# Building a selector matrix earlier on the Pool engine, and reordering two kinds of DMA on SyncE, in a sliding-window attention and GeGLU kernel

## The chip, the cores and the metric

The kernel runs on one core of a Trainium2 chip. The metric is the device time in microseconds (us) of one execution. Before the change three runs gave 400.01, 400.31 and 400.64 us; their median is 400.31 us. One further execution was recorded by the hardware profiler; all rows of the profile come from that one.

## The reference

For 8 batches of 8 heads, 576 positions and head size 64 the reference computes causal attention in a window of 128 positions with a linear (ALiBi) bias, and feeds the result, 4608 tokens of 512, through a gated feed-forward layer:

```python
scores = scale * np.matmul(q, k.transpose(0, 1, 3, 2))
mask = (rel >= 0) & (rel < window)                  # window = 128
scores = np.where(mask, scores + bias[None], -1e9)
attn = softmax(scores)
x = np.matmul(attn, v)  ->  (4608, 512)
g, val = x @ w_gate, x @ w_val                      # (512, 1536) each
out = (gelu(g) * val) @ w_out                       # (1536, 512)
```

Inputs and output are 32-bit floats in DRAM.

## The kernel before

**Loads.** The Pool engine issues all loads (`load`, `load_w`): five DMAs for each of q, k and v of a batch, which convert to bf16 on the way, and the weights, in four slices of 384 columns each for the gate (`wg`) and the value (`wv`) matrix, then two pieces of `wo`. The buffers `qs`, `ks`, `vb` exist twice; batch b uses number b mod 2, so a load of batch b + 2 waits until batch b has been read.

**Transposes.** q and k are needed with the head dimension on the partitions (`qT`, `kT`). Batches 0 and 1 are transposed by TensorE through an identity matrix (`transpose`, line 105). Batches 2 to 7 are transposed by two DMAs that SyncE issues (`transposes_dma`, line 113).

**Attention.** `scores2` and `scores` compute keys times queries (line 121), ScalarE takes the exponential (line 128), VectorE multiplies a mask with the bias in it (line 131). `sums` adds the probabilities of each query with a matrix of ones (line 176), and VectorE takes the reciprocal into `sumrow`, a tile "r" (line 185). The reciprocal has to be spread over 64 partitions for each head, into a tile "rb". For batches 0 to 3 TensorE does this with the selector matrix `sel` (`spread_pe`, matmul at line 199 and copies at line 206). For batches 4 to 7 DMAs do it: one writes r to a DRAM tile "rd", two read it back broadcast (`spread_dma`, lines 189 and 191). `values` multiplies the probabilities with v (line 217), and VectorE multiplies by rb into `xT` (line 223).

**Feed-forward.** A group g is 512 tokens; there are nine. `gate_val` does eight matmuls for one of 12 blocks of 128 hidden columns (line 236), gelu on ScalarE (line 240) and the product on VectorE (line 241). `out_half` does six matmuls for half of the contraction of 128 tokens (line 252); after the second half ScalarE copies the result into a tile "osb" (line 257) and SyncE sends it out (line 259). The pool of osb has three buffers. All PSUM tiles come in turn from one pool of eight banks: `gate_val` takes two banks for each block, `out_half` one for two halves.

**Order.** The order of instructions on each engine is the order in which the program is written (`manual_schedule`); each engine works its list from the front, and an instruction whose operand is not ready holds everything behind it on that engine. The same is so for the lists of DMAs on SyncE and Pool. The first batch's attention is written out by hand, then comes a loop over the groups: `transposes_dma(g + 2)` and `load_v(g + 2)`, the 12 blocks of `gate_val`, `load_qk(g + 3)`, and then the eight halves of `out_half` mixed with the attention of coming batches by the lists `todo` and `steps`. In groups 3 to 6 `sums` and `spread_dma` of batch g + 1 stand behind block 0, and its `values` behind blocks 8 and 10.

Of the kernel before, what the change touches and what calls it, by code (L numbers as in the profile page):

```python
# [10 lines left out]
ALU = mybir.AluOpType  # L11
# [15 lines left out]
def kernel(  # L27
# [10 lines left out]
    nc = tc.nc  # L38
    B, H, S, D = q.shape
# [23 lines left out]
    def bank():  # L63
        return psum.tile([128, 512], FP32, name="ps")
# [8 lines left out]
    sel = consts.tile([128, 2, 64], FP32, name="sel")  # L73
# [7 lines left out]
    def load(t, src, b, js=range(5)):  # L81
        for j in js:
            lo = 64 if j == 0 else 0
            nc.gpsimd.dma_start(  # L84
                out=t[lo:128, j, :].rearrange("p (h d) -> p h d", h=H),
                in_=src[b][:, 128 * j - 64 + lo:128 * j + 64, :].rearrange("h p d -> p h d"))

    def load_qk(b):
        load(qs[b % 2], q, b)
        load(ks[b % 2], k, b)  # L90

    def load_v(b):
        load(vb[b % 2], v, b)
# [7 lines left out]
    def transpose(b, what, c, js, ps):  # L101

        src, dst = ((ks, kT), (qs, qT))[what]
        for n, j in enumerate(js):
            nc.tensor.transpose(  # L105
                out=ps[:, 128 * n:128 * n + 128],
                in_=src[b % 2][:, j, 128 * c:128 * c + 128], identity=ident)
        return (dst[b % 2][:, js[0]:js[0] + len(js), c, :],
                ps[:, 0:128 * len(js)].rearrange("p (j t) -> p j t", t=128))

    def transposes_dma(b):
        for src, dst in ((ks, kT), (qs, qT)):
            nc.sync.dma_start_transpose(  # L113
                out=dst[b % 2].rearrange("p j c t -> p (j c) t"),
                in_=src[b % 2].rearrange("p j x -> p (j x)"))
# [29 lines left out]
    def scores(b, s, cs):  # L145

        pss = []
        for c in cs:
            ps = [bank(), bank()]
            pss.append(ps)  # L150
            for j, blocks, col in (((0, (0, 1), 0), (1, (1, 2), 256)),
                                   ((4, (4,), 0), (2, (3,), 128), (3, (3, 4), 256)))[s]:
                for i in (0, 1):
                    score(b, c, i, j, blocks, ps[i], col)
        for c, ps in zip(cs, pss):
            P = p_pool[s].tile([128, 2, 512], BF16, name="P")
            probs[b, s, c] = P
            for i in (0, 1):
                exp(P[:, i, :], ps[i])
            mask(P.rearrange("p i (n x) -> p i n x", n=2),  # L160
                 emask[:, 2 * c:2 * c + 2, :].unsqueeze(2).to_broadcast((128, 2, 2, 256)))
# [8 lines left out]
    def sums(b, s):  # L170

        ps = bank()
        for j, a, e in PIECES[s]:
            for i in (0, 1):
                for c in range(4):
                    nc.tensor.matmul(  # L176
                        out=ps[32 * c:32 * c + 32, a:e],
                        lhsT=ones[:, min(j, 1), i, :], rhs=prob(b, s, c, i, j, e - a),
                        start=(i == 0 and j == 2 * s), stop=(i == 1 and j == 2 * s + 2),
                        skip_group_check=True)  # L180
        if s == 0:
            sumrow[b] = r_pool.tile([128, S], FP32, name="r")
            recip[b] = r_pool.tile([128, 4, S], FP32, name="rb")
        lo, hi = PART[s]
        nc.vector.reciprocal(sumrow[b][:, lo:hi], ps[:, 0:hi - lo])  # L185

    def spread_dma(b):
        d = d_pool.tile([4, 2, S], FP32, name="rd")
        nc.sync.dma_start(out=d.rearrange("c i s -> (c i) s"), in_=sumrow[b][0:128:16, :])
        for i in (0, 1):  # L190
            nc.sync.dma_start(
                out=recip[b][64 * i:64 * i + 64, :, :],
                in_=d[:, i, :].unsqueeze(0).to_broadcast((64, 4, S)))
# [14 lines left out]
    def values(b, s, cs):  # L208
        lo, hi = PART[s]
        pss = []  # L210
        for c in cs:
            ps = bank()
            pss.append(ps)
            for j, a, e in PIECES[s]:
                for i in (0, 1):
                    h = 2 * c + i
                    nc.tensor.matmul(  # L217
                        out=ps[64 * i:64 * i + 64, a:e],
                        lhsT=vb[b % 2][:, j, 64 * h:64 * h + 64],
                        rhs=prob(b, s, c, i, j, e - a),  # L220
                        start=(j == 2 * s), stop=(j == 2 * s + 2), skip_group_check=True)
        for c, ps in zip(cs, pss):
            nc.vector.tensor_tensor(  # L223
                out=xT[:, c, b * S + lo:b * S + hi], in0=ps[:, 0:hi - lo],
                in1=recip[b][:, c, lo:hi], op=ALU.mult)
# [3 lines left out]
    def gate_val(g, f, lo=0, hi=512):  # L229
        if g not in hid:  # L230
            hid[g] = h_pool.tile([128, NF, 512], BF16, name="hT")
        t0 = 512 * g
        pg, pv = bank(), bank()
        for w, ps in ((wg, pg), (wv, pv)):
            for c in range(4):
                nc.tensor.matmul(  # L236
                    out=ps[:, 0:hi - lo], lhsT=w[:, c, 128 * f:128 * (f + 1)],
                    rhs=xT[:, c, t0 + lo:t0 + hi], start=(c == 0), stop=(c == 3))
        gl = g_pool.tile([128, 512], BF16, name="gelu")
        nc.scalar.activation(out=gl[:, 0:hi - lo], in_=pg[:, 0:hi - lo], func=AF.Gelu)  # L240
        nc.vector.tensor_tensor(out=hid[g][:, f, lo:hi], in0=pv[:, 0:hi - lo],  # L241
                                in1=gl[:, 0:hi - lo], op=ALU.mult)
# [20 lines left out]
    for t in qs + ks:  # L263
        nc.vector.memset(t[0:64, 0, :], 0.0)
    nc.gpsimd.affine_select(
        out=ident, in_=ident, compare_op=ALU.not_equal, fill=1.0,
        base=0, pattern=[[-1, 128]], channel_multiplier=1)
# [3 lines left out]
    for half, base, step, chan in ((0, 0, 1, -1), (1, -1, -1, 1)):  # L271
        t = tmpl[:, 128 * half:128 * half + 128]
        nc.gpsimd.affine_select(
            out=t, in_=t, compare_op=ALU.is_ge, fill=1e9,
            base=base, pattern=[[step, 128]], channel_multiplier=chan)
    for js in ((0, 1, 2), (3, 4)):
        for j in js:
            for t, src in ((qs[0], q), (ks[0], k)):
                load(t, src, 0, (j,))
    load_v(0)  # L280
    step = DFF // 4
    for n in range(4):
# [5 lines left out]
    for i in range(2):  # L288
        nc.vector.memset(ones[64:128, 0, i, 16 * i:16 * i + 16], 1.0)
        nc.vector.memset(ones[:, 1, i, 16 * i:16 * i + 16], 1.0)  # L290
    nc.vector.memset(sel, 0.0)
    for i in range(2):
        nc.vector.memset(vb[i][0:64, 0, :], 0.0)
    for h in range(H):
# [10 lines left out]
    for (w, c), ps in pss.items():  # L305
        (act, dve)[w](out=(kT, qT)[w][0][:, 0:3, c, :],
                      in_=ps[:, 0:384].rearrange("p (j t) -> p j t", t=128))
# [10 lines left out]
    scores(0, 0, (2, 3))  # L318
    rest((2, 3), dve)
    scores(0, 1, (0, 1))  # L320
    for c in range(4):
        nc.gpsimd.affine_select(  # L322
            out=sel, in_=sel, compare_op=ALU.not_equal, fill=1.0,
            base=-32 * c, pattern=[[-16, 2], [0, 64]], channel_multiplier=1)
    sums(0, 0)
    scores(0, 1, (2, 3))
    spread_pe(0, 0)
# [9 lines left out]
    for n in range(2):  # L337
        nc.gpsimd.dma_start(
            out=wo[:, 6 * n:6 * n + 6, :],
            in_=moe_w_out[768 * n:768 * n + 768, :].rearrange("(c p) f -> p c f", p=128))  # L340
# [20 lines left out]
    def steps(g):  # L361
        b = g + 2
        if g in todo:
            return todo[g]
        if b >= B:
            return range(8)
        return [("s2", b), ("s", b, 0, (0, 1)), 0, 1, ("s", b, 0, (2, 3)), 2, 3,
                ("s", b, 1, (0, 1)), 4, 5, ("s", b, 1, (2, 3)), 6, 7]
# [3 lines left out]

    for g in range(NG):
        if g + 2 < B:
            transposes_dma(g + 2)
            load_v(g + 2)
        for f in range(3 if g == 0 else 0, NF):
            gate_val(g, f)
            if g == 0 and f >= 8:
                for w in (0, 1):  # L380
                    o, i = transpose(1, w, f - 8, range(5), bank().bitcast(BF16))
                    (act, dve)[w](out=o, in_=i)  # L382
            if 3 <= g < B - 1:
                if f == 0:
                    sums(g + 1, 0)
                    sums(g + 1, 1)
                    spread_dma(g + 1)
                elif f in (8, 10):
                    for s in (0, 1):
                        values(g + 1, s, (f - 8, f - 7))  # L390
        if g + 3 < B:
            load_qk(g + 3)
        for item in steps(g):
            if isinstance(item, int):
                out_half(g, item)
            else:
                RUN[item[0]](*item[1:])
# [30 lines left out]
```

## Time and profile before

| what | value |
|---|---|
| median of three runs | 400.31 us |
| the profiled execution's own time | 402.94 us |
| its span, first to last instruction | 401.1 us |
| TensorE matmuls (PE) busy | 352.8 us, 88% |
| VectorE (DVE) busy | 188.4 us, 47% |
| ScalarE (ACT) busy | 187.7 us, 47% |
| GpSimd (POOL) busy | 110.9 us, 28% |
| share of the chain that ended last: PE / DMA / ACT / POOL | 76% / 7% / 6% / 5% |

A row of the timeline has the start and length in us, the engine, the line, the operation with output and inputs, and the count; in brackets stands how long the engine was idle before it and what ended that. "SPq" is the list of DMAs on SyncE: the length of a row there is how long SyncE was held by issuing, and landing comes later. A row of the waits has who waited for whom, the total in us, the number of times and the longest. A row of the DMA view has output and input, the issuing list, the number, the size and the median us from issue to landing. A row of the windows has a stretch, its length, each engine's busy us with a count, the clock that TensorE was granted (1.00 is full), the busy share of the DMA engines and GB/s.

### The profile page before, as it was taken

The page shows a single profiled execution, that of the slowest core. Times are in us where ns is not written, and L with a number is a line of the kernel's source. Part 1 is how long each engine was busy: PE and PEld are TensorE (multiplying, and loading weights), DVE is VectorE, ACT ScalarE, POOL GpSimd, SP SyncE. Part 2 cuts the span into 40 slices and gives each one's busy share as a digit, 9 for nine tenths or more (in the row PEclk, how much of TensorE's full clock was granted, in tenths as well). Part 3 has the DMA queues.
Part 4 walks back from the last instruction along what each step waited for, and adds up shares of the span by engine and source line. Part 5 has one row for each costly group of instructions (what it writes and reads, how often), then busy time and mean ns, then how long its engine had stood idle before and what let it go on. Part 6 is the DMA issues. An engine that isn't in the chain of part 4 may idle for free.

```text
span 401.1 us, 6564 instructions
## 1 busy us (share of the span) xinstructions
PE 352.8 (88%) x2616; PEld 172.4 (43%) x2616; DVE 188.4 (47%) x308; ACT 187.7 (47%) x337; POOL 110.9 (28%) x142
## 2 busy tenths in 40 slices
PE   2700899879998999899959999999999999999996
PEld 1500555444444444444434445444444444444442
DVE  2630544483448744877344556464556521321420
ACT  3820334844368644676308633953584222323321
POOL 9945864727300560173029002100000000000000
PEclk9955799999999999999978999999999999999999
DMA  9999999999991899299949983977020502002002
GB/s 69 148 202 163 147 163 180 141 98 134 134 91 54 80 151 134 38 114 150 148 94 150 175 173 41 104 133 171 2 78 32 117 26 78 2 27 79 2 4 100
DMA packets 156863, 41.40 MB, mean 103 GB/s; under 512 B 144512, under 2 KB 150144, under 8 KB 156832
## 3 DMA queue, kind: packets, MB, share of 16 engines
q0 software_dynamic: 118304, 18.88, 65.0%
q1 hardware_dynamic: 38528, 22.10, 26.1%
q8 instruction: 20, 0.33, 0.3%
q14 instruction: 11, 0.09, 0.1%
HBM read 42.47 MB, written 9.51 MB: 130 GB/s over the span
## 4 chain that ended last, share of the span: by engine, by line
PE 76%; DMA 7%; ACT 6%; POOL 5%; DVE 2%; SPq 2%; issue 1%; POOLq 0%; DVEq 0%; ACTq 0%
PE ps L236 43%; PE ps L252 22%; PE ps L217 4%; ACT P L128 4%; DMA wv<-in_moe_w_val_dram 4%; PE ps L121 3%; DMA rb<-rd 2%; SPq L113 2%; PE ps L176 2%; PE ps L199 2%; POOL ks L84 1%; POOL qs L84 1%; POOL vb L84 1%; ACT L128 1%; DVE r L185 1%
## 5 line engine op out<-in xcount | busy, mean ns | idle before, releaser
L241 DVE TENSOR_TENSOR hT<-ps,gelu 128x512 bf16<-128x512 f32 (+2 forms) x111 | 74.2, 674 | 122.7 <-PE ps L236 110.7
L240 ACT ACTIVATE gelu<-ps 128x512 bf16<-128x512 f32 (+2 forms) x111 | 64.9, 586 | 126.1 <-PE ps L236 123.7
L236 PE MATMUL ps<-xT,wg 128*128 128x512 bf16 (+2 forms) x444 | 113.2, 377 | 0.5 <-DVE xT L223 0.2
L236 PE MATMUL ps<-xT,wv 128*128 128x512 bf16 (+2 forms) x444 | 112.3, 376 | 0.0
L252 PE MATMUL ps<-wo,hT 128*128 128x512 bf16 x432 | 99.5, 380 | 0.0
L128 ACT ACTIVATE P<-ps 128x512 bf16<-128x512 f32 x144 | 74.3, 629 | 9.7 <-PE ps L121 9.6
L131 DVE TENSOR_TENSOR P<-P,emask 128x1024 bf16<-128x1024 bf16 x72 | 49.0, 686 | 36.9 <-ACT P L128 36.6
L84 POOL DMA_DIRECT2D vb<-in_v_dram x40 | 33.7, 868 | 116.9 <-PE ps L217 116.8
L236 PEld LDWEIGHTS <-wv 128*128 128x128 bf16 x444 | 43.5, 98 | 51.0 <-issue 1.3
L236 PEld LDWEIGHTS <-wg 128*128 128x128 bf16 x444 | 42.2, 98 | 49.4 <-issue 1.9
L252 PEld LDWEIGHTS <-hT 128*128 128x128 bf16 x432 | 39.6, 98 | 48.8 <-issue 4.4
L257 ACT COPY osb<-ps 128x512 f32<-128x512 f32 x36 | 21.7, 602 | 40.1 <-PE ps L252 34.3
L84 POOL DMA_DIRECT2D qs<-in_q_dram x40 | 34.0, 874 | 19.7 <-PE ps L105 7.4
L84 POOL DMA_DIRECT2D ks<-in_k_dram x40 | 34.1, 895 | 3.5 <-DMA wv<-in_moe_w_val_dram 2.1
L185 DVE RECIPROCAL r<-ps 128x320 f32<-128x320 f32 (+1 forms) x16 | 30.7, 1938 | 0.9 <-PE ps L176 0.9
L199 PE MATMUL ps<-r,sel 32*128 32x320 f32 (+1 forms) x64 | 6.8, 493 | 25.8 <-POOL sel L322 21.0
L223 DVE TENSOR_TENSOR xT<-ps,rb 128x320 bf16<-128x320 f32 (+1 forms) x64 | 24.8, 449 | 9.2 <-DMA rb<-rd 9.2
L121 PE MATMUL ps<-qT,kT 64*128 64x256 bf16 (+1 forms) x384 | 24.2, 255 | 0.7 <-DVE qT L382 0.4
L217 PE MATMUL ps<-P,vb 128*64 128x128 bf16 (+2 forms) x384 | 19.9, 258 | 4.5 <-DVE xT L223 4.5
L217 PEld LDWEIGHTS <-vb 128*64 128x64 bf16 x384 | 16.2, 117 | 11.5 <-issue 11.3
L121 PEld LDWEIGHTS <-kT 64*128 64x128 bf16 x384 | 13.7, 97 | 15.0 <-issue 12.5
L206 ACT COPY rb<-ps 128x320 f32<-128x320 f32 (+1 forms) x16 | 5.7, 417 | 24.6 <-PE ps L199 24.6
(37 smaller groups left out, 93.1 us busy)
## 6 DMA issues: line engine op xcount, KB each, us to landing
out_dram<-osb SPq DMA_DIRECT2D x36, 256.0 KB, 2.1
rb<-rd SPq DMA_DIRECT2D x8, 576.0 KB, 7.1
qs<-in_q_dram POOLq DMA_DIRECT2D x32, 128.0 KB, 5.5
ks<-in_k_dram POOLq DMA_DIRECT2D x32, 128.0 KB, 6.0
vb<-in_v_dram POOLq DMA_DIRECT2D x32, 128.0 KB, 4.3
wg<-in_moe_w_gate_dram POOLq DMA_DIRECT2D x4, 384.0 KB, 11.9
wv<-in_moe_w_val_dram POOLq DMA_DIRECT2D x4, 384.0 KB, 13.1
wo<-in_moe_w_out_dram POOLq DMA_DIRECT2D x2, 768.0 KB, 9.3
```

Source lines behind the costliest of these rows:

```text
L84: nc.gpsimd.dma_start(out=t[lo:128, j, :].rearrange("p (h d) -> p h d", h=H), in_=src[b][:, 128 * j - 64 + lo:128 * j + 64, :].rearrange(" ...
L121: nc.tensor.matmul(out=ps[:, col:col + 128 * n].rearrange("p (n t) -> p n t", n=n), lhsT=kT[b % 2][lo:lo + 64, j, c, :], rhs=qT[b % 2][lo: ...
L128: nc.scalar.activation(out=dst, in_=src, func=AF.Exp, scale=0.125)
L131: nc.vector.tensor_tensor(out=dst, in0=dst, in1=m, op=ALU.mult)
L185: nc.vector.reciprocal(sumrow[b][:, lo:hi], ps[:, 0:hi - lo])
L217: nc.tensor.matmul(out=ps[64 * i:64 * i + 64, a:e], lhsT=vb[b % 2][:, j, 64 * h:64 * h + 64], rhs=prob(b, s, c, i, j, e - a), start=(j == ...
L223: nc.vector.tensor_tensor(out=xT[:, c, b * S + lo:b * S + hi], in0=ps[:, 0:hi - lo], in1=recip[b][:, c, lo:hi], op=ALU.mult)
L236: nc.tensor.matmul(out=ps[:, 0:hi - lo], lhsT=w[:, c, 128 * f:128 * (f + 1)], rhs=xT[:, c, t0 + lo:t0 + hi], start=(c == 0), stop=(c == 3))
L240: nc.scalar.activation(out=gl[:, 0:hi - lo], in_=pg[:, 0:hi - lo], func=AF.Gelu)
L241: nc.vector.tensor_tensor(out=hid[g][:, f, lo:hi], in0=pv[:, 0:hi - lo], in1=gl[:, 0:hi - lo], op=ALU.mult)
L252: nc.tensor.matmul(out=po, lhsT=hid[g][:, f, 128 * t:128 * (t + 1)], rhs=wo[:, f, :], start=(f == 0), stop=(f == NF - 1))
L257: nc.scalar.copy(out=osb, in_=po)
```

## The change

Two independent edits. The first builds `sel` (a zero fill on VectorE and four `affine_select` on Pool) right behind the loads of q and k of batch 0, ahead of the loads of v and the weights; before, the four stood on Pool behind all weights and the q and k loads of batch 1. The second leaves the order in groups 0 to 2 as it is, but in groups 3 to 5 writes `transposes_dma(g + 2)` behind `spread_dma(g + 1)` instead of at the head of the group. No instruction is added or removed.

```diff
             for t, src in ((qs[0], q), (ks[0], k)):
                 load(t, src, 0, (j,))
+    nc.vector.memset(sel, 0.0)
+    for c in range(4):
+        nc.gpsimd.affine_select(
+            out=sel, in_=sel, compare_op=ALU.not_equal, fill=1.0,
+            base=-32 * c, pattern=[[-16, 2], [0, 64]], channel_multiplier=1)
     load_v(0)
...
-    nc.vector.memset(sel, 0.0)
...
     scores(0, 1, (0, 1))
-    for c in range(4):
-        nc.gpsimd.affine_select(
-            out=sel, in_=sel, compare_op=ALU.not_equal, fill=1.0,
-            base=-32 * c, pattern=[[-16, 2], [0, 64]], channel_multiplier=1)
     sums(0, 0)
...
         if g + 2 < B:
-            transposes_dma(g + 2)
+            if g < 3:
+                transposes_dma(g + 2)
             load_v(g + 2)
...
                     spread_dma(g + 1)
+                    if g + 2 < B:
+                        transposes_dma(g + 2)
```

On Pool, at the start of the program (qs_94, ks_96 and vb_102 are the buffers of batch 0, ks_97 and vb_103 of batch 1), the two places of the difference are these:

```order
 L84 DMA qs_94<-in_q_dram 128x8x64
 L84 DMA ks_96<-in_k_dram 128x8x64
+L282 AFFINE_SELECT sel<-sel 128x128 x4
 L84 DMA vb_102<-in_v_dram 64x8x64
 L84 DMA vb_102<-in_v_dram 128x8x64 x4
```

and, 23 DMAs further down,

```order
 L84 DMA ks_97<-in_k_dram 64x8x64
 L84 DMA ks_97<-in_k_dram 128x8x64 x4
-L322 AFFINE_SELECT sel<-sel 128x128 x4
 L338 DMA wo<-in_moe_w_out_dram 128x6x512 x2
 L84 DMA vb_103<-in_v_dram 64x8x64
```

The four selects moved past 23 DMAs: the five of v, the eight of wg and wv and the ten of q and k of batch 1.

On SyncE, from the outputs of group 2 to those of group 3, the list before is:

```order
L259 DMA out_dram<-osb 128x512 x4
L113 DMA_TRANSPOSE kT_101<-ks_97 128x20x128
L113 DMA_TRANSPOSE qT_99<-qs_95 128x20x128
L189 DMA rd<-r 8x576
L191 DMA rb<-rd 64x4x576 x2
L259 DMA out_dram<-osb 128x512 x4
```

and with the change:

```order
L259 DMA out_dram<-osb 128x512 x4
L189 DMA rd<-r 8x576
L191 DMA rb<-rd 64x4x576 x2
L113 DMA_TRANSPOSE kT_101<-ks_97 128x20x128
L113 DMA_TRANSPOSE qT_99<-qs_95 128x20x128
L259 DMA out_dram<-osb 128x512 x4
```

The three DMAs that spread the reciprocal now stand ahead of the two transposes, which therefore also stand behind the spread's waits: for the reciprocal, and for rd to land. Groups 4 and 5 change in the same way; group 6 has no transposes and stays.

## The prediction

> **What bounds the kernel now.** I read the page's shares first: TensorE is busy 88% of the span, and its chain covers 76%. Only its idle time and its slow time can be won. The list of waits names the two idle times that this change touches.
>
> ```profile
> span 401.1 us, 6564 instructions
> PE ps L199 <- POOL sel L322: 21.0, 1, 21.0
> DVE xT L223 <- DMA rb<-rd: 9.2, 3, 7.8
> PE ps L217 <- DVE xT L223: 4.5, 1, 4.5
> ```
>
> One wait of 21.0 us is for the selector; one of 4.5 us is for a multiply that itself waits for rb. The second edit can touch three groups (3, 4, 5), but only one of them stops TensorE. The timeline (PE, DVE, POOL, then the chain) shows the first wait.
>
> ```profile
> 19.40 0.74 PE L121 MATMUL ps<-qT,kT 64*128 64x128 bf16 x12
> 41.11 1.45 PE L199 MATMUL ps<-r,sel 32*128 32x320 f32 x8 [20.97 <-POOL sel L322]
> 42.49 2.13 PE L217 MATMUL ps<-P,vb 128*64 128x192 bf16 x24
> 64.70 0.44 PE L105 MATMUL ps<-ident,ks 128*128 128x128 bf16 x5
> ...
> 20.85 2.15 DVE L185 RECIPROCAL r<-ps 128x320 f32<-128x320 f32 x1
> ...
> 39.64 1.42 POOL L322 TENSOR_SCALAR_AFFINE_SELECT sel<-sel 128x128 f32<-128x128 f32 x4
> ...
> 20.04 16.70 DMA wv<-in_moe_w_val_dram
> ```
>
> The matmul needs r and sel. r is ready at 20.85 + 2.15 = 23.00; sel comes at 41.1 because its four instructions stand behind loads that wait for weights still landing.
>
> **Edit one: sel earlier.** The selects now stand 23 DMAs ahead, long before 23.0, so what ends last is the reciprocal. The matmul starts at 23.04 (r plus 0.04 of hand-over), not 41.11: **18.07 us** sooner. I then asked what is late next.
>
> *Weights and k.* The selects hold Pool 1.42 us, so each load behind them lands at most 1.42 later, until the place they left, which gives the 1.42 back ahead of wo. These rows give the tightest cases, first the start of wv's first slice, then issue to landing of that slice and of a piece of k of batch 1:
>
> ```profile
> 15.63 0.86 POOL L97 DMA_DIRECT2D wv<-in_moe_w_val_dram  x1
> ...
> wv<-in_moe_w_val_dram POOLq DMA_DIRECT2D x1, 384.0 KB, 9.6
> ...
> ks<-in_k_dram POOLq DMA_DIRECT2D x1, 128.0 KB, 5.6
> ```
>
> The first wv slice lands at 15.63 + 9.6 + 1.42 = 26.7. Its first user follows the spread by 2.13 + 1.45 us of older matmuls and four of its own block, so not before 27. The last wv piece lands at 20.04 + 16.70 + 1.42 = 38.2; its user, block 9, stands behind the first transposes on TensorE, at 64.70 - 18.07 = 46.6. Those transposes need the last piece of k, issued at 38.75 (ahead of the selects, 0.89 before 39.64): 38.75 + 5.6 + 1.42 = 45.8, 0.8 early. Nothing is lost, on paper: 0, with a bound of +1.5.
>
> *The clock.* The windows show what idleness does to TensorE's clock.
>
> ```profile
> 21.00:22.00 1.00, 0.00 (x0) 0.00 (x0) 1.00 (x1) 1.00 (x3) 0.00 (x0) 0.73 1.30 198
> ...
> 45.00:46.00 1.00, 1.00 (x7) 0.66 (x6) 0.16 (x1) 0.31 (x1) 1.00 (x3) 0.82 1.22 194
> ```
>
> Work ended at 20.14; the granted clock drops within 21 to 22 and returns within 45 to 46, about 4.3 us after work resumed. That slow work is paid either way if the remaining gap, 20.14 to 23.04, still drops it; the history up to 22 is the same, so I take no gain. The Trainium skill ("TensorE: Matmul & The Clock Gate", Part 1: The HAM clock gate) says that the clock is halved after an idle window of about 3.4 us and that the windows run free. By that rule a gap of 2.9 us need not halve it. The trace differs here: it fell some 1.4 us into the gap. Bound: -2.0 us, since half of 4.3 us at half clock would be won.
>
> *SyncE's list at the end of group 0.* TensorE comes 18 us sooner to the outputs; SyncE does not. Its first two entries are the transposes of batch 2, and behind them stand the outputs of group 0.
>
> ```profile
> 64.93 3.92 SPq L113 DMA_TRANSPOSE kT<-ks  x1
> 79.55 16.84 SPq L259 DMA_DIRECT2D out_dram<-osb  x4
> 96.61 5.55 SPq L113 DMA_TRANSPOSE kT<-ks  x1
> 102.33 8.52 SPq L113 DMA_TRANSPOSE qT<-qs  x1
> ...
> 72.35 4.20 POOL L84 DMA_DIRECT2D qs<-in_q_dram  x5 [7.44 <-PE ps L105]
> ...
> 95.44 0.59 ACT L257 COPY osb<-ps 128x512 f32<-128x512 f32 x1 [3.12 <-issue]
> ...
> 95.36 19.87 PE ps L236 x92
> ...
> out_dram<-osb SPq DMA_DIRECT2D x1, 256.0 KB, 6.0
> ...
> qT<-qs SPq DMA_TRANSPOSE x1, 14.0
> ```
>
> The transposes of batch 2 start when its k has landed, at 64.93; that follows Pool's loads and stays near 65. But the loads of batch 3, held until 72.35 by TensorE's transposes, now run on at once and collide with them. The pair at 96.61, beside such loads, held SyncE for 5.55 + 8.52 us and some 0.2 between. So the first output, ready at 79.55 - 18.07 = 61.5, is issued at about 65 + 14.3 = 79.3 and lands 6.0 later (the out row, beside loads), at 85.3. The fourth osb copy, due at 95.44 - 18.07 = 77.4, reuses the first one's buffer (three exist) and waits until then; ScalarE's gelus queue behind it. TensorE goes on from 77.2 with the banks it has: 28 matmuls at 19.87 / 92 = 0.216, to 83.2; the next needs the bank that the copy frees at 85.9: 2.7 us idle. Then the first gelu (1.28 of table loading and 0.60, as at the other group starts) lets it wait another 0.8. I take **+3.5**. Below: 0, where SyncE is held for about 8 us as at 64.93. Above: the last transpose lands 14.0 after its issue and the output behind it, copy at 88.6, with a clock drop: +9.
>
> **Edit two: the spread ahead of the transposes.** Group 3 (DVE, SPq, chain, PE) and, for comparison, group 4:
>
> ```profile
> 185.10 3.76 DVE L185 RECIPROCAL r<-ps 128x320 f32<-128x320 f32 x2
> ...
> 181.17 7.19 SPq L113 DMA_TRANSPOSE kT<-ks  x1
> 188.53 6.84 SPq L113 DMA_TRANSPOSE qT<-qs  x1
> 195.46 0.71 SPq L189 DMA_DIRECT2D rd<-r  x1
> ...
> 198.36 7.92 DMA rb<-rd
> ...
> 201.44 1.03 PE L236 MATMUL ps<-xT,wv 128*128 128x512 bf16 x4
> 206.95 2.02 PE L217 MATMUL ps<-P,vb 128*64 128x192 bf16 x24 [4.48 <-DVE xT L223]
> 212.43 0.90 PE L121 MATMUL ps<-qT,kT 64*128 64x128 bf16 x16
> ...
> 228.97 3.76 DVE L185 RECIPROCAL r<-ps 128x320 f32<-128x320 f32 x2
> ...
> 227.01 3.21 SPq L113 DMA_TRANSPOSE kT<-ks  x1
> 230.32 3.06 SPq L113 DMA_TRANSPOSE qT<-qs  x1
> ...
> 247.00 1.13 PE L217 MATMUL ps<-P,vb 128*64 128x192 bf16 x24
> 249.90 0.83 PE L121 MATMUL ps<-qT,kT 64*128 64x128 bf16 x16
> ...
> kT<-ks SPq DMA_TRANSPOSE x1, 5.2
> ...
> qT<-qs SPq DMA_TRANSPOSE x1, 5.5
> ```
>
> r is ready at 188.86, but SyncE is held by transposes until 195.37; rb lands at 206.28, and TensorE stands from 202.47 to 206.95. With the spread first, rd goes out at 188.9 and rb lands 206.28 - 195.46 = 10.8 later, at 199.7: the stop of 4.48 goes. So does the slow work behind it: from the second values to the scores it took 212.43 - 206.95 = 5.48 in group 3 and 249.90 - 247.00 = 2.90 in group 4, the same instructions. Together 4.48 + 2.58 = **7.06 us** sooner. In groups 4 and 5 rb already stops nothing.
>
> What is late next: kT and qT, whose first user is the scores of batch g + 2 (212.43 - 7.06 = 205.37 in group 3). Undisturbed, a pair lands about 3.3 + 5.5 = 8.8 after its first issue (230.32 - 227.01, and the last row, qT of group 0; kT of group 4 took 5.2), of which I put down 2 as start-up, from rd: 195.46 to the next issue at 197.64, leaving 6.8 of moving. I estimate that it moves behind rb: group 3: 188.9 + 10.8 + 6.8 = 206.5, late by 1.2. Group 4: 232.73 + 10.8 + 6.8 = 250.35 against 249.90, late by 0.45; group 5 is built alike, 0.45. Sum **+2.1**. Below 0, since the 2 us are rough; above, the pair as slow as at 96.61, in the rivals.
>
> **Sum.** 402.94 - 18.07 + 3.5 - 7.06 + 2.1 = 383.4 for an execution like the profiled one. The runs' median was 2.63 below it: **380.8 us**.
>
> **Rivals.**
>
> (a) *No new wait* at either place: 380.8 - 5.6 = 375.2. For it: both are worked out from rows with other neighbours. Against it: the loads do move up. 0.15.
>
> (b) *The clock stays full* through the 2.9 us gap: 378.8. 0.10; the row at 21 to 22 speaks against it.
>
> (c) *The jam at the end of group 0 at its upper bound*, 9 instead of 3.5: 386.3. 0.15.
>
> (d) *The wait moves*: rb and the transposes share the engines instead of queueing. rb has some 6 us of moving, of which about 1.6 are done when the transposes start; 4.4 at half speed lands it 4.4 later, at 204.1 in group 3 and 248.0 in group 4. TensorE resumed 0.67 after rb (206.95 against 206.28), so it stops 2.3 us in group 3 (from 202.47) and some 1.6 each in groups 4 and 5: 5.5 instead of 2.1, and with a clock drop of 2.6 or two: 384 to 389. 0.07. The Trainium skill ("DMA: Bandwidth & Descriptors", Queues, rings and completion order) says that each DMA engine consumes one issuer's descriptors in ring order, which speaks against (d); no row here isolates it.
>
> (e) *Slower*: the transposes late in all of groups 3, 4 and 5. If each pair took what the one at 96.61 took, 102.33 + 14.0 - 96.61 = 19.7 instead of 8.8, the scores would wait 10.9 more and run into a slow clock (2.6), three times: 380.8 + 40.5 = 421. The change turns slower once a pair exceeds about 13 us. Against it: Pool's loads for batch g + 3 are mostly done when these transposes now start. 0.03.
>
> **How the numbers follow.** My forecast case holds 0.50. Faster by over 0.2% (what a measurement of this kernel can tell from no change) holds in all but (e): 0.96 with a little of (e)'s lower end; same 0.01; slower 0.03. The range 375 to 388 takes in (a), (b), (c) and most of (d).
>
> **What would show it.** Right: no wait on sel; the first line 199 at 23; a wait of the fourth osb copy for an output DMA near 77; no wait of line 223 for rb in group 3; short waits of line 121 for the transposes in groups 3 to 5. Wrong: TensorE waiting for wv or k between 26 and 47, a stop at the values of groups 3 to 5, or long waits at the scores.

## The result, and the profile after

The changed kernel ran in 382.25 us (median of 4 executions, 380.54 to 383.15), the kernel before in 400.48 (4 executions, 400.01 to 400.93): a ratio of 0.954, 95% interval 0.9501 to 0.9579. The forecast was 380.8, within 375 to 388. The profiled execution of the changed kernel took 382.87 us. One of the later executions of the kernel before took 410.91 us in a slower state of the chip; the ratios and ranges below leave it out.

The list of waits of the changed kernel shows what has gone and what has come (who waits for whom, total, times, longest):

```profile
PE ps L199 <- DVE r L185: 5.2, 3, 3.0
...
PE ps L236 <- ACT osb L257: 2.5, 1, 2.5
```

The wait of 21.0 us for `sel` is gone; line 199 now waits 3.0 us at most, for the reciprocal. TensorE's wait of 4.5 us at line 217 is gone. Two waits of TensorE are new: 2.5 us behind a copy into osb, which itself waited 10.9 us for an output DMA, and 0.5 us for a transpose (the rows of these come further down).

The timeline of the changed kernel, PE from the first spread on:

```profile
23.00 1.45 PE L199 MATMUL ps<-r,sel 32*128 32x320 f32 x8 [3.00 <-DVE r L185]
...
36.57 1.03 PE L236 MATMUL ps<-xT,wg 128*128 128x512 bf16 x4
46.93 0.44 PE L105 MATMUL ps<-ident,ks 128*128 128x128 bf16 x5
```

The spread starts at 23.00 instead of 41.11. The first transposes of batch 1 start at 46.93 instead of 64.70.

The same timeline at the end of group 0, SPq, ACT and PE:

```profile
65.79 5.88 SPq L113 DMA_TRANSPOSE kT<-ks  x1
71.84 6.92 SPq L113 DMA_TRANSPOSE qT<-qs  x1
78.82 7.60 SPq L259 DMA_DIRECT2D out_dram<-osb  x4
...
85.48 0.59 ACT L257 COPY osb<-ps 128x512 f32<-128x512 f32 x1 [10.92 <-DMA out_dram<-osb]
...
82.61 1.03 PE L236 MATMUL ps<-xT,wg 128*128 128x512 bf16 x4
86.11 1.87 PE L236 MATMUL ps<-xT,wv 128*128 128x512 bf16 x4 [2.48 <-ACT osb L257]
88.02 1.69 PE L236 MATMUL ps<-xT,wg 128*128 128x512 bf16 x4
89.55 1.03 PE L236 MATMUL ps<-xT,wv 128*128 128x512 bf16 x4
```

SyncE is held by the two transposes of batch 2 from 65.79 to 78.76 and issues the outputs of group 0 only then. The fourth copy into osb, which needs the first one's buffer, stands until 85.48. TensorE stops for 2.48 us and then runs two rows at about half speed.

And in group 3, SPq and PE:

```profile
175.47 0.71 SPq L189 DMA_DIRECT2D rd<-r  x1
...
178.89 6.89 SPq L113 DMA_TRANSPOSE kT<-ks  x1
185.94 3.64 SPq L113 DMA_TRANSPOSE qT<-qs  x1
...
188.97 1.13 PE L217 MATMUL ps<-P,vb 128*64 128x192 bf16 x24
191.87 0.83 PE L121 MATMUL ps<-qT,kT 64*128 64x128 bf16 x16
```

The spread goes out ahead of the transposes, the values start without a wait, and from there to the scores it takes 191.87 - 188.97 = 2.90 us, the time that group 4 took before the change.

### The profile page after: what moved, and what is told of

It reads as the page before. It is cut to its first block, busy times and chain, and to the rows that moved or that the text cites. A ratio compares the mean times of both kernels' runs of the same rounds, so it can differ in the third digit from the quotient of the medians.

```text
span 381.1 us, 6564 instructions
## 1 busy us (share of the span) xinstructions
PE 352.0 (92%) x2616; PEld 171.7 (45%) x2616; DVE 188.1 (49%) x308; ACT 187.3 (49%) x337; POOL 110.8 (29%) x142
## 4 chain that ended last, share of the span: by engine, by line
PE 80%; ACT 8%; DMA 4%; DVE 3%; POOL 2%; issue 1%; SPq 1%; POOLq 0%; ACTq 0%; DVEq 0%
PE ps L236 46%; PE ps L252 22%; ACT P L128 5%; PE ps L217 4%; PE ps L121 3%; PE ps L176 2%; DMA out_dram<-osb 2%; PE ps L199 2%; DVE r L185 2%; DMA qT<-qs 1%; DMA ks<-in_k_dram 1%; POOL qs L84 1%; PE ps L105 1%; ACT L128 1%; DVE P L131 1%; POOL ks L84 1%
## 5 line engine op out<-in xcount | busy, mean ns | idle before, releaser
L217 PE MATMUL ps<-P,vb 128*64 128x128 bf16 (+2 forms) x384 | 19.0, 251 | 0.0
L217 PEld LDWEIGHTS <-vb 128*64 128x64 bf16 x384 | 15.3, 113 | 7.0 <-issue 6.9
L105 PE MATMUL ps<-ident,ks 128*128 128x128 bf16 x40 | 6.3, 260 | 9.8 <-DMA ks<-in_k_dram 9.6
```

Source lines behind the costliest of these rows:

```text
L217: nc.tensor.matmul(out=ps[64 * i:64 * i + 64, a:e], lhsT=vb[b % 2][:, j, 64 * h:64 * h + 64], rhs=prob(b, s, c, i, j, e - a), start=(j == ...
```

## The experiments

"After" is the changed kernel. The first four runs were compared with the kernel before on one chip (median 400.99 us there), the last four on another (400.89 us). After itself was not run again beside them, so a difference from its 382.25 us carries the half microsecond by which the medians of the kernel before differ (400.48 to 400.99).

### Each edit alone

The first edit alone keeps `transposes_dma(g + 2)` at the head of every group:

```diff
-            if g < 3:
-                transposes_dma(g + 2)
+            transposes_dma(g + 2)
...
-                    if g + 2 < B:
-                        transposes_dma(g + 2)
```

> The first edit alone: sel early, the DMAs on SyncE in the old order. My theory: TensorE waits 3.0 us for the reciprocal at 23 instead of 21.0 for sel, the fourth osb copy still waits about 11 us for the first output, TensorE loses about 4.3 us there (2.5 idle, the rest at half clock), and the stop of about 4.5 us with its slow tail (7.1 in all) stays in group 3. From the changed kernel's 382.25: + 7.1 - 0.5 = 388.8; from the kernel before, 400.4 - 18.1 + 4.3 = 386.6. Rival: the two edits are not independent, and the stop in group 3 goes away, or moves, by the shift alone: then about 382.

Measured: 388.04 us (386.54 to 388.68), ratio 0.9682 (0.9643 to 0.9721). Its list of waits:

```profile
ACT osb L257 <- DMA out_dram<-osb: 9.5, 1, 9.5
...
PE ps L217 <- DVE xT L223: 4.1, 1, 4.1
```

The jam at osb comes with the first edit; the stop at the values of group 3 (4.1 us) stays.

The second edit alone is the kernel before with the loop's new order of `spread_dma` and `transposes_dma`, `sel` left where it was:

```diff
             if g + 2 < B:
-                transposes_dma(g + 2)
+                if g < 3:
+                    transposes_dma(g + 2)
...
                     spread_dma(g + 1)
+                    if g + 2 < B:
+                        transposes_dma(g + 2)
```

> The second edit alone: sel late as before, the spread ahead of the transposes in groups 3 to 5. My theory: the wait of 21 us for sel stays, no jam at the end of group 0, no stop in group 3, at most 0.5 us of waiting at the scores of group 4: 400.4 - 7.06 + 0.5 = 393.8. Rival: the stop in group 3 is longer in the profiled execution (2.6 us above the median) than in a timed one, and the gain is only about 4.5: 396.

Measured: 394.7 us (394.38 to 396.46), ratio 0.9862 (0.9823 to 0.9902). From its list of waits:

```profile
PE ps L199 <- POOL sel L322: 19.4, 1, 19.4
```

The wait for `sel` stands, and that list has no wait of line 257 for an output DMA and none of line 217 for line 223.

Alone the edits gain 400.99 - 388.04 = 12.95 and 400.99 - 394.7 = 6.29, 19.24 together; both in one kernel gain 400.48 - 382.25 = 18.23. The two places are independent to within about a microsecond, which is what the medians scatter by.

### The jam at the end of group 0

Is the new wait of TensorE at 86 really caused by the third buffer of osb, and by SyncE held beside the loads? Two runs take away one cause each. The first gives the pool of osb a fourth buffer, so that the fourth copy needs no output to have landed:

```diff
-    o_pool = ctx.enter_context(tc.tile_pool(name="op", bufs=3))
+    o_pool = ctx.enter_context(tc.tile_pool(name="op", bufs=4))
```

> The changed kernel with a fourth osb buffer. My theory: what TensorE lost at the start of group 1 came from the fourth copy's wait for the first output's buffer, and nothing else waits for these outputs: the wait of 10.9 us on ScalarE goes, with the 2.5 us of idle TensorE and the half clock behind it, 382.25 - 4.3 = 377.9. Rival: the copy was only the first in line, and gelu or a later copy meets SyncE's hold anyway: 381 to 382.

Measured: 377.51 us (377.29 to 378.07), ratio 0.9428 (0.939 to 0.9467, clear of after's interval): 4.74 us below after. Its timeline, SPq and ACT:

```profile
64.99 4.90 SPq L113 DMA_TRANSPOSE kT<-ks  x1
70.06 7.43 SPq L113 DMA_TRANSPOSE qT<-qs  x1
77.55 2.19 SPq L259 DMA_DIRECT2D out_dram<-osb  x4
...
77.14 0.59 ACT L257 COPY osb<-ps 128x512 f32<-128x512 f32 x1 [3.07 <-PE ps L252]
```

SyncE is held about as long as in after (4.90 + 7.43), and it no longer matters: the fourth copy waits for TensorE's result alone.

The second leaves three buffers and moves the loads of q and k of batch 3 behind the load of v, in group 1, so that they don't run beside the transposes of batch 2:

```diff
+            if g == 1:
+                load_v(3)
+                load_qk(3)
...
-            load_v(g + 2)
+            if g != 1:
+                load_v(g + 2)
...
-        if g + 3 < B:
+        if 0 < g and g + 3 < B:
```

> The changed kernel with three osb buffers, but the q and k loads of batch 3 moved behind the v loads of batch 3 (which wait for TensorE), so that they no longer run beside the transposes of batch 2. My theory: it was the collision that made these transposes hold SyncE for 13 us; alone they hold it for about 7.5 (3.92 + 3.58 before the change), the first output is issued near 73.5 and lands before the fourth copy is due at 77.6: 377.9. Rival: the place in SyncE's list is enough, the hold stays about 13 us without those loads: 382.

Measured: 378.21 us (377.23 to 379.16), ratio 0.9441 (0.9403 to 0.948, clear of it too): 4.04 us below after. Its timeline, SPq and ACT:

```profile
64.86 4.16 SPq L113 DMA_TRANSPOSE kT<-ks  x1
69.19 4.48 SPq L113 DMA_TRANSPOSE qT<-qs  x1
73.72 4.19 SPq L259 DMA_DIRECT2D out_dram<-osb  x4
...
76.97 0.59 ACT L257 COPY osb<-ps 128x512 f32<-128x512 f32 x1 [3.12 <-PE ps L252]
```

Without the loads beside them the same two transposes hold SyncE for 8.8 us (64.86 to 73.67) instead of 13.0, the outputs go out 5 us sooner, and three buffers are enough. So the jam needs both: too few buffers for the time that SyncE is held, and loads that lengthen that time.

### The clock in the gap before the first spread

The remaining runs stand on the version with four buffers, called "four" below. This one fills the gap ahead of the first spread with 13 matmuls that nobody reads, to keep TensorE's clock full:

```diff
     scores(0, 1, (2, 3))
+    warm = bank()
+    for n in range(13):
+        nc.tensor.matmul(
+            out=warm, lhsT=ident, rhs=emask[:, 0:2, :].rearrange("p h n -> p (h n)"),
+            start=True, stop=True)
     spread_pe(0, 0)
```

> The kernel with four osb buffers (377.51) and 13 extra matmuls of 512 columns (some 2.8 us) on TensorE in the gap between the last scores at 20 and the spread at 23; their result is not used. My theory: the gap drops the clock, and the first 3.4 to 6.8 us of work after 23 run at half speed; filled, the clock stays full and the work behind it ends 1.7 to 2.4 sooner, less some tenths if the extra work runs past 23: 375.1 to 376.0. Rival: the drop comes from the thin work before 20, not from the gap, and the slow stretch stays: 377.5 or a little more.

Measured: 377.66 us (376.86 to 378.32), ratio 0.9422 (0.9399 to 0.9444), against 377.51 for "four": no gain, where 375.1 to 376.0 was expected. The timeline (PE) and a window of the profiled execution show what happened. In a windows row the clock stands before the DMA share and the GB/s:

```profile
20.21 2.75 PE L329 MATMUL ps<-emask,ident 128*128 128x512 bf16 x12 [0.16 <-issue]
23.06 0.82 PE L199 MATMUL ps<-r,sel 32*128 32x320 f32 x8
...
35.48 1.03 PE L236 MATMUL ps<-xT,wg 128*128 128x512 bf16 x3
...
65.57 1.45 PE L199 MATMUL ps<-r,sel 32*128 32x320 f32 x8 [2.01 <-ACT P L128]
```

```profile
65.00:67.00 2.00, 1.43 (x10) 0.60 (x12) 1.57 (x3) 0.47 (x2) 2.00 (x4) 0.65 2.28 145
```

The filling works where it stands: the eight matmuls of the first spread take 0.82 us, against 1.45 in after, and no drop follows. In "four", the kernel that was filled, they took 0.82 us too, and the clock fell behind them (the window from 24 to 26 reads 0.54). From the spread to the first 512-wide gate matmul it takes 35.48 - 23.06 = 12.42 us. In the profiled execution of "four" the same stretch took 36.08 - 23.20 = 12.88 us, so the gain at that place is 0.46 us; against after (36.57 - 23.00 = 13.57) it is 1.15. From the timeline (PE) of "four":

```profile
23.20 0.82 PE L199 MATMUL ps<-r,sel 32*128 32x320 f32 x8 [2.29 <-DVE r L185]
...
36.08 1.03 PE L236 MATMUL ps<-xT,wg 128*128 128x512 bf16 x4
```

And the filled execution halved the clock further down, behind the 2.01 us of idleness ahead of 65.57, where "four" kept it full. So the filling decides only one of the places where the clock can drop.

Two of the four executions of the filled kernel had a mean granted clock of 1.000 and took 376.86 and 377.07; two had 0.995 and took 378.25 and 378.32. It is tempting to read a price of about 1.3 us for one dropped clock from these, but the four of the run with the loads moved don't sort so (378.90 at 1.000, 377.23 to 379.16 at 0.995), and the mean can hide a drop. The timeline (PE) and a window of the last run but one below, whose mean is 1.000 as well, show it:

```profile
22.98 1.45 PE L199 MATMUL ps<-r,sel 32*128 32x320 f32 x8 [2.23 <-DVE r L185]
...
37.17 1.03 PE L236 MATMUL ps<-xT,wg 128*128 128x512 bf16 x3
```

```profile
22.00:24.00 2.00, 1.02 (x8) 0.55 (x8) 1.97 (x3) 0.41 (x1) 0.85 (x2) 1.00 1.30 203
```

The window reads 1.00, yet the eight matmuls take 1.45 us as at half clock. That trace's clock records begin only at 29.21 us, and the profile counts what lies ahead of them as full. Its stretch to the first 512-wide gate matmul is the longest of all, 37.17 - 22.98 = 14.19 us.

### The reciprocal, sooner

With `sel` in time the first spread waits for the reciprocal. On "four", this run computes it ahead of the masks of the next scores, by splitting `scores` into matmuls, exponentials and masks (the three new functions are left out here):

```diff
-    scores(0, 1, (0, 1))
+    pss = score_mm(0, 1, (0, 1))
     sums(0, 0)
-    scores(0, 1, (2, 3))
+    score_exp(0, 1, (0, 1), pss)
+    pss = score_mm(0, 1, (2, 3))
+    score_exp(0, 1, (2, 3), pss, masked=False)
     spread_pe(0, 0)
     values(0, 0, range(4))
+    for c in (2, 3):
+        score_mask(0, 1, c)
```

> The kernel with four osb buffers (377.51), and VectorE's reciprocal of the first half (2.15 us) written ahead of the masks of the second half, two of which come behind the first multiplies now. My theory: the reciprocal is what ends the gap, so it starts at 19.4 instead of 20.7 and the spread at 21.6 instead of 23.0: 376.1, and up to 2 us less where the shorter gap keeps the clock: 374 to 376. Rival: the next wait takes its place at once, the first wv slice (lands near 26.1, used from 27.5) or k of batch 1 (45.4 against 46.9) bounds the gain to about 1: 376.5 to 377.5.

Measured: 376.88 us (5 executions, 376.15 to 377.94), ratio 0.941 (0.9389 to 0.9431). The timeline, PE (these line numbers are 10 higher in this kernel):

```profile
21.98 1.27 PE L209 MATMUL ps<-r,sel 32*128 32x320 f32 x8 [1.67 <-DVE r L195]
...
34.88 1.03 PE L246 MATMUL ps<-xT,wg 128*128 128x512 bf16 x3
```

The profiled execution starts the spread 1.22 us sooner than "four" and reaches the first 512-wide gate matmul at 34.88, 1.20 us sooner than the 36.08 of "four". The medians differ by 0.63 and the intervals overlap, so this gain is not told apart from none; 376.1 was expected, and the rival's 376.5 to 377.5 holds the measured time. It is the version with the lowest median: 5.37 us below the changed kernel, nearly all of it from the fourth buffer.

### Do rb and the transposes share the DMA engines?

The rival (d) of the prediction said that rb moves slower when the transposes are queued right behind it. This run, on "four", leaves out the DMA transposes of batches 5 to 7:

```diff
                     spread_dma(g + 1)
-                    if g + 2 < B:
-                        transposes_dma(g + 2)
```

> The kernel with four osb buffers, with the DMA transposes of batches 5 to 7 left out (their scores are computed from what the buffers held, so the output of these batches is not the reference's). It measures whether transposes queued behind the spread slow it down. If rb and the transposes go one after the other (my forecast's estimate), rb lands as long after rd's issue as with them, about 10 us in groups 3 to 5. If they share the engines, rb lands about 4.4 us sooner than with them: about 10 with them, 6 without. The end: within 0.5 us of 375.6, the profiled execution with four buffers.

Measured, a single execution: 378.35 us, a span of 376.6 us where 375.6, give or take 0.5, was expected. It lost 14.19 - 12.88 = 1.31 us against "four" in the slow stretch at its start, shown above, which lies ahead of every transpose that was left out. What bears on (d) is group 3. First the timeline (SPq, DVE) of "four":

```profile
170.59 0.71 SPq L189 DMA_DIRECT2D rd<-r  x1
...
181.01 1.55 DVE L223 TENSOR_TENSOR xT<-ps,rb 128x320 bf16<-128x320 f32 x4 [0.67 <-DMA rb<-rd]
```

then the timeline (SPq) of this run, and from its DMA view the second piece of rb (number, size, us from issue to landing):

```profile
171.68 0.71 SPq L189 DMA_DIRECT2D rd<-r  x1
...
174.27 0.60 SPq L191 DMA_DIRECT2D rb<-rd  x1
...
rb<-rd SPq DMA_DIRECT2D x1, 576.0 KB, 7.1
```

With the transposes behind it rb was there 181.01 - 170.59 = 10.4 us after rd's issue, without them 174.27 + 7.1 - 171.68 = 9.7. In group 4 it came 223.78 - 212.13 = 11.65 us after it in the profile of after, and 9.9 in this run. So the transposes that are queued behind rb cost it 0.7 us where one edit alone separates the kernels, and up to 1.7 with other differences, where (d) needed 4.4 in every group. Rival (d) falls in its size: rb is not slowed as by an equal share. The Trainium skill ("DMA: Bandwidth & Descriptors", Queues, rings and completion order) has one issuer's descriptors consumed in ring order on each DMA engine; the small cost agrees with it, and where the 0.7 us comes from stays open.

### What the selects cost the loads

Here, on "four", the four selects stand behind the weight loads instead of ahead of them, so that v and the weights go out 1.4 us sooner:

```diff
-    nc.vector.memset(sel, 0.0)
-    for c in range(4):
-        nc.gpsimd.affine_select(...)
     load_v(0)
     ...
         load_w(step * n, step * (n + 1))
+    nc.vector.memset(sel, 0.0)
+    for c in range(4):
+        nc.gpsimd.affine_select(...)
```

> The kernel with four osb buffers (377.51), and the four selects on Pool behind the weight loads instead of ahead of the v loads, still ahead of q and k of batch 1: they run near 21 to 22.4. My theory: sel is still ready before the reciprocal (23.0), and loads 1.4 us sooner help nothing since no one waits for them: 377.5, no change. Rival: weights or k were late by some tenths in the changed kernel, and it gains up to 1: 376.5; or sel, at 22.4 plus Pool's waits, is late: 378 and more.

Measured: 377.72 us (377.1 to 378.25), ratio 0.9424 (0.9403 to 0.9444): the same as "four". The timeline, POOL and PE:

```profile
20.75 1.65 POOL L286 TENSOR_SCALAR_AFFINE_SELECT sel<-sel 128x128 f32<-128x128 f32 x4
...
23.37 1.45 PE L199 MATMUL ps<-r,sel 32*128 32x320 f32 x8 [3.00 <-DVE r L185]
```

Even here the selects end at 22.40, ahead of the reciprocal at 23.3, and the spread still waits for r. Neither of these two places costs anything that can be measured; what cost 18 us before was the one behind the loads of batch 1 too, which wait for weights to land.

## Why the prediction was right, step by step

The sum ran 402.94 - 18.07 + 3.5 - 7.06 + 2.1 = 383.4 for a profiled execution, less 2.63 for the median. Each term against the profile of after:

| term | predicted | measured | from |
|---|---|---|---|
| wait for `sel` | -18.07 | -18.11 | 41.11 to 23.00 |
| weights, k of batch 1 | 0 (up to +1.5) | 0 | no such wait of TensorE |
| clock in the shorter gap | 0 (down to -2.0) | +0.34 | 13.23 to 13.57, see below |
| jam at the end of group 0 | +3.5 | +4.34 | see below |
| stop and slow clock in group 3 | -7.06 | -7.06 | no wait; 2.90 to the scores |
| transposes late, groups 3 to 5 | +2.1 | +0.5 | waits of line 121 |
| sum, profiled execution | 383.4 | 382.95 | the execution took 382.87 |
| to the median | -2.63 | -0.62 | 382.87 to 382.25 |

*Wait for `sel`.* Right, and for the reason given: what ends last is the reciprocal.

*Weights and k.* Right: TensorE waits for none of them, and the run with the selects behind the weight loads shows that their 1.4 us of Pool cost nothing that can be measured.

*Clock.* The prediction took the drop as unchanged. These windows of after, at the first gap, show it:

```profile
21.00:22.00 1.00, 0.00 (x0) 0.00 (x0) 1.00 (x1) 1.00 (x3) 1.00 (x2) 0.57 1.25 177
...
27.00:28.00 1.00, 1.00 (x6) 0.56 (x5) 0.04 (x1) 0.28 (x1) 0.34 (x1) 0.52 1.32 204
```

TensorE's work ended at 20.00 and the clock fell between 21 and 22, although the gap is 3.0 us now and was 21.0. Rival (b), the clock staying full, falls for this execution. What the slow stretch costs differs by execution: from the first spread to the first 512-wide gate matmul, which stood at this start before,

```profile
54.34 1.03 PE L236 MATMUL ps<-xT,wg 128*128 128x512 bf16 x4
```

it took 54.34 - 41.11 = 13.23 us before, 13.57 after, 12.88 in "four", 14.19 without the last transposes, and 12.42 with the gap filled. A full clock there is worth 0.5 to 1.8 us, within the bound of 2.0, and 1.15 in the profile of after.

*The jam.* The prediction had the outputs issued at 79.3, the copy freed at 85.3 and TensorE idle for 2.7 us; it was 78.82, 85.48 and 2.48. Behind that it put a wait of 0.8 us for the first gelu. There was none. The clock took its place, as the windows of after show:

```profile
86.00:88.00 2.00, 1.87 (x4) 0.56 (x4) 0.00 (x0) 1.97 (x4) 0.47 (x1) 0.50 2.03 200
88.00:90.00 2.00, 1.98 (x7) 0.76 (x7) 2.00 (x4) 1.69 (x4) 1.91 (x3) 0.65 2.43 155
```

The rows of four such matmuls ahead of the stop, at full clock, start 0.865 us apart (six of them from 77.42 to 82.61), so the one at 89.55 would have stood at 82.61 + 3 x 0.865 = 85.21: 4.34 us lost, 2.48 of them idle and the other 1.86 in the slow rows behind. Taking the jam away gave 4.74 (fourth buffer) and 4.04 (loads moved), which shows the mechanism. Its size is not the same in every profile. In the profile of the first edit alone the clock stayed full, and there the wait for the first gelu is seen (timeline, PE):

```profile
85.08 1.02 PE L236 MATMUL ps<-xT,wv 128*128 128x512 bf16 x4 [1.08 <-ACT osb L257]
87.00 1.02 PE L236 MATMUL ps<-xT,wg 128*128 128x512 bf16 x4 [0.89 <-ACT gelu L240]
```

The row ahead of these starts at 82.97, so the one at 87.00 would have stood at 82.97 + 2 x 0.865 = 84.70: 2.3 us lost. The gelu wait of the prediction was thus right in kind, and in after the slower matmuls covered it; the +3.5 lies between two profiled executions of 2.3 and 4.3. Rival (a), no new wait, falls here; rival (c), 9 us, too.

*Group 3.* Right to the hundredth by the profile, and the second edit alone gave 6.29 against -7.06 + 0.5 = -6.56.

*Transposes late.* This term was mis-sized. The only wait is in group 4, from the timeline of after:

```profile
229.83 0.84 PE L121 MATMUL ps<-qT,kT 64*128 64x128 bf16 x16 [0.50 <-DMA qT<-qs]
```

The prediction let the pair move 6.8 us behind rb, rb itself landing 10.8 after rd's issue. In group 3 of after the timeline (DVE) and the DMA view (median us from issue to landing) have

```profile
185.75 1.55 DVE L223 TENSOR_TENSOR xT<-ps,rb 128x320 bf16<-128x320 f32 x4 [0.52 <-DMA rb<-rd]
```

```profile
qT<-qs SPq DMA_TRANSPOSE x1, 5.3
```

so rb was there at about 185.7, 10.2 after rd's issue at 175.47, and the second transpose, issued at 185.94, landed at 191.2: 5.5 behind rb, and 0.6 ahead of its user at 191.87. The pair moved 1.3 us faster than estimated, and rb came 0.6 sooner than the one whose rows the prediction used. In group 4 the wait came out at 0.50 against 0.45, but with rb some 0.8 later and the pair some 0.8 faster than estimated, which is luck; in group 5 there was no wait. The errors of the terms, +0.84 for the jam, +0.34 for the clock and -1.6 here, cancel in part too, so that their sum fits better than its parts. Rival (e), 10.9 late three times, was far off.

*From the sum to the median.* This was the weakest step, and it makes up most of the miss. The execution profiled before lay 2.63 us above its median; the prediction subtracted that from a sum that had been made from that execution. But the distance of one execution from the median is no property of the kernel: it was +2.63 for the one before (402.94, while the executions of that kernel in the comparisons lie between 399.0 and 401.75), +0.62 for after and -1.50 for the first edit alone (386.54 against 388.04). The miss of 382.25 - 380.8 = 1.45 is 2.0 from here, less 0.5 from the terms. What made that one execution longer stays open.

## What to carry to other kernels

Move an instruction ahead of a queue when the row of its consumer shows that only this queue holds it, and then read the queues again at the new times: here TensorE came 18 us sooner to a SyncE that didn't, and a fourth output buffer gave back 4.7 us. On a queue that issues long transposes, put what has a waiting reader first; the transposes behind it lost 0.5 us where the reader won 7. And make the sum against the execution whose rows it uses, but let its distance from the median widen the range instead of shifting the forecast.

## What the runs showed of the hardware

**The clock falls after less idleness than a window.** The granted clock goes down and up in stretches that are multiples of 3.4 us: in after it is low from 21.1 (0.57 of 21 to 22 means 0.86 us at half) to 27.96, which is 6.8 us, and again from 86.0 to 89.4 (0.65 of 88 to 90 means 1.4 us at half). It fell in the three profiled drops read here within or right behind idle times of 3.00, 2.48 and 2.01 us, each shorter than one such stretch. In the 3.41 us that end at the first of these drops TensorE was busy for more than half:

```profile
17.73:21.14 3.41, 1.93 (x48) 1.24 (x42) 3.18 (x9) 3.29 (x8) 3.41 (x6) 1.00 1.59 136
```

The Trainium skill ("TensorE: Matmul & The Clock Gate", Part 1: The HAM clock gate) gives a free-running window of about 3.4 us, with which the lengths agree, and puts the drop after at least one idle window, with which this row does not: no window that ends there was idle throughout. The phase matters: the two drops of after, at 21.14 and 86.0, lie nineteen times 3.41 us apart, as if the windows ran on through the work between. Counted so, one ends at 65.5 in after, in the middle of the idle time of 2.01 us that ends at 66.66, and the clock stayed full; in the filled run one ends at 65.6 (0.65 of 65 to 67 means 1.4 us at half), right behind the same idle time, and the clock halved. How much of a window has to be idle is not shown: 1.93 busy us of 3.41 did not keep the clock up above, while in the run with the reciprocal sooner 1.63 busy us did, from 63.19 to 66.60, a window counted on in the same way from that run's drop at 22.2.

**SyncE is held longer by a transpose when loads run beside it.** The transposes of batch 2 held it 4.16 + 4.48 us with the loads of batch 3 moved away and 5.88 + 6.92 beside them; moving those loads is the only edit between the two kernels.
